# First unit of a fused attention, MLP and gated-convolution kernel in one written order, with whole float32 weights in its second layer

## The chip, the cores and the metric

The kernel runs on one core of a Trainium2 chip. The metric is the device time of one launch in microseconds: a median of 1182.4 us over three runs, from 1181.29 to 1183.06. The engines are named TensorE (PE in the rows; PEld are its weight loads), VectorE (DVE), ScalarE (ACT), GpSimd (POOL) and SyncE (SP, which issues the transfers).

## The reference

```python
# x (8, 8, 512, 64): batch, head, token, d; state (8, 8, 32, 64)
scores = x @ state.T / 8;  xread = softmax(scores) @ state          # tokens read the state
scores2 = state @ x.T / 8; sread = softmax(scores2) @ x             # the state reads the tokens
x = concat([xread, sread], axis=2)    # 544 rows per head, then the heads side by side: (8, 544, 512)
xn = (x - mean) / sqrt(var + 1e-6) * g_ln
x = x + relu(xn @ w_ch1) @ w_ch2      # w_ch1 (512, 2048), w_ch2 (2048, 512), read as below
h = relu(x @ w_in)                    # w_in (512, 1024)
out = h * sigmoid(conv3(h, conv_w)) @ w_out
```

`x`, `state` and the result are float32. The three weight matrices and `conv_w` arrive as float64 and are rounded to float32 on the chip before use.

## The kernel before

The work on the batch is cut into units. Units 0 to 7 are the 512 tokens of one batch element each; a unit numbered 8 holds the 256 state rows of all of them and runs before the last. A unit's layers are tiled into 16 slices `m` of 128 hidden columns. `L1(u, m)` is the first layer of a slice: since the tokens are weighted sums of 32 state rows per head, it multiplies the token weights (`AH`, `AL`) with the state already multiplied into the weights (`Z`), not the 512-column rows. `z_tiles` makes that `Z` from the state and a folded quarter `j` of w_ch1. `relu_parts` takes the ReLU out of the PSUM bank `ph` on ScalarE (`hH`, line 633) and its remainder on VectorE (`hL`, line 634). `L2(u, m, n)` adds the slice into the four PSUM banks `acc`; `residual` scales them by the norm's `rstd` and adds the tokens. For a product close to float32, `three` (lines 619 to 621) multiplies a high and a low part held as fp32r: high by high, high by low, low by high.

The weights arrive as raw 64-bit words. `round_1` (two ScalarE passes) and `round_2` (two VectorE passes, lines 205 and 206, here called a rounding pair, and a GpSimd addition, line 207) make float32 of them; `Converter.third` splits a rounded w_ch2 slice into its two parts, on ScalarE (line 239) and GpSimd (line 240). All 32 pieces (16 of w_ch1, 16 of w_ch2) are converted in the first unit, through three temporaries: `ctmp0`, `ctmp1` and a part of `XTt`. In that unit `z_first(j)` also folds the norm into a quarter of w_ch1: four float32 products with `gmean` on TensorE (line 609), four VectorE corrections (line 612), then the z products (line 585), and a store of the folded quarter to `w1d` in DRAM. Later units load it back through a ring of seven buffers (`pass_pairs`).

Beside a unit's products run the tasks of the next: `token_norm` of this unit, then `attend` of the next (scores, two softmaxes, state reads, token reads), one step in each gap between slices.

The order is set in two ways. The first steps (`START`) and everything from the second unit to the first steps of the last part are issued as written. The first unit's body is arranged by a scheduler, which moves instructions of different slices past each other on each engine's queue. A piece is converted when a product needs it, four places ahead (`need`, `AHEAD`).

## Time and profile before

| | us |
|---|---|
| median of three runs | 1182.4 |
| profiled execution | 1177.81 |
| its span, first to last instruction | 1176.0 |
| TensorE busy | 1125.9 (96%) |
| VectorE busy | 726.6 (62%) |
| ScalarE busy | 444.2 (38%) |
| GpSimd busy | 207.8 (18%) |

The profiled execution is 4.6 us shorter than the median of the timed runs; a difference between the kernels is worked out on the profiled one and then taken off the median. In the page's view of 40 slices of 29.4 us each, TensorE is busy for five to eight tenths of the first four slices and nine or more of nearly all others; GpSimd works in the first five slices and again in the last part alone. Shares of busy time over the whole span say little here, since the first 173 us and the rest have different limits.

### The profile page before, as it was taken

Reading aid. Unit: us, or ns where it says so; the run is one execution under the profiler, and the core shown is the slowest. Engines: PE = TensorE matmul, PEld = TensorE weight load, DVE = VectorE, ACT = ScalarE, POOL = GpSimd, SP = SyncE. Lnnn points to the kernel's source line nnn. Section 1 sums busy time; section 2 is a strip of 40 time slices with the busy share of each in tenths; the row PEclk is TensorE's granted clock in tenths of the full one; section 3 lists DMA queues with packets and bytes.
Section 4 is the critical chain, followed back from the end, with each engine's and each line's share of the span. In section 5 each row is a group of like instructions: output and inputs, shape, how many; then the busy total and the mean of one; then the engine's idle time right before and its main releaser. Section 6 shows DMA issues by size and latency. Waiting matters only on the chain.

```text
span 1176.0 us, 14628 instructions
## 1 busy us (share of the span) xinstructions
PE 1125.9 (96%) x5459; PEld 863.8 (73%) x5459; DVE 726.6 (62%) x1134; ACT 444.2 (38%) x788; POOL 207.8 (18%) x314
## 2 busy tenths in 40 slices
PE   5698899999999999999989999999999999999997
PEld 4365567777777777777767888788788888888885
DVE  4899666566566475565665622577677666666553
ACT  5665333323233233233233222565344434334332
POOL 2565400000000000000000000265433312213110
PEclk8699999999999999999999999999999999999999
DMA  9643533432243333334314124322112102100001
GB/s 298 206 171 108 158 96 105 108 95 90 72 109 85 81 111 76 78 120 108 95 56 107 38 101 155 119 72 90 37 54 72 37 37 80 37 36 36 1 37 45
DMA packets 129283, 106.31 MB, mean 90 GB/s; under 512 B 103332, under 2 KB 107452, under 8 KB 128188
## 3 DMA queue, kind: packets, MB, share of 16 engines
q1 hardware_dynamic: 129212, 105.37, 29.6%
q8 instruction: 43, 0.70, 0.2%
q14 instruction: 28, 0.23, 0.1%
HBM read 83.85 MB, written 21.50 MB: 90 GB/s over the span
## 4 chain that ended last, share of the span: by engine, by line
PE 80%; DVE 12%; ACT 3%; issue 2%; POOL 2%; SPq 0%; DMA 0%; ACTq 0%; DVEq 0%; POOLq 0%
PE acc L619 14%; PE acc L620 14%; PE acc L621 14%; PE ph L619 7%; PE ph L620 7%; PE ph L621 7%; PE pat L585 2%; PE pat L621 2%; PE pat L619 2%; PE pat L620 2%; PE pat L361 2%; PE ph L647 2%; DVE tn L500 1%; ACT bQ L488 1%; DVE ctmp L206 1%
## 5 line engine op out<-in xcount | busy, mean ns | idle before, releaser
L619 PE MATMUL acc<-hH,w 128*128 128x512 f32 (+1 forms) x576 | 221.6, 395 | 2.2 <-ACT hH L633 2.2
L620 PE MATMUL acc<-hL,w 128*128 128x512 f32 (+1 forms) x576 | 220.4, 383 | 1.8 <-DVE hL L634 1.7
L621 PE MATMUL acc<-hH,w 128*128 128x512 f32 (+1 forms) x576 | 220.1, 382 | 0.0
L634 DVE SCALAR_TENSOR_TENSOR hL<-ph,hH 128x512 fp32r<-128x512 f32 (+1 forms) x144 | 94.2, 657 | 183.4 <-ACT hH L633 183.2
L633 ACT ACTIVATE hH<-ph 128x512 fp32r<-128x512 f32 (+1 forms) x144 | 81.6, 569 | 208.9 <-PE ph L621 171.3
L619 PEld LDWEIGHTS acc<-hH,w 128*128 128x128 f32 x576 | 108.1, 188 | 54.5 <-issue 15.9
L1008 DVE SCALAR_TENSOR_TENSOR w<-w,cw,w 128x544 f32<-128x544 f32 x128 | 109.9, 860 | 38.0 <-POOL w L1006 36.2
L620 PEld LDWEIGHTS acc<-hL,w 128*128 128x128 f32 x576 | 109.2, 190 | 24.3 <-DVE hL L634 4.2
L621 PEld LDWEIGHTS acc<-hH,w 128*128 128x128 f32 x576 | 109.0, 189 | 21.7
L207 POOL TENSOR_TENSOR ctmp<-ctmp,AH 128x512 int32<-128x512 int32 x1 | 1.3, 1304 | 610.7 <-DVE ctmp L206 610.7
L619 PE MATMUL ph<-AH,ZH 128*128 128x512 f32 x256 | 104.3, 408 | 0.7 <-ACT ZH L594 0.7
L620 PE MATMUL ph<-AL,ZH 128*128 128x512 f32 x256 | 100.9, 394 | 0.0
L621 PE MATMUL ph<-AH,ZL 128*128 128x512 f32 x256 | 100.1, 395 | 0.0
L989 ACT ACTIVATE w<-w 128x544 f32<-128x544 f32 x64 | 42.1, 657 | 129.4 <-DVE w L1008 129.4
L996 DVE TENSOR_TENSOR w<-w,w 128x512 fp32r<-128x512 f32 x64 | 49.5, 774 | 42.9 <-ACT w L995 42.1
L990 DVE TENSOR_TENSOR w<-w,w 128x544 f32<-128x544 f32 x64 | 48.8, 762 | 39.5 <-ACT w L989 39.5
L619 PEld LDWEIGHTS ph<-AH,ZH 128*128 128x128 f32 x256 | 48.5, 190 | 19.5 <-issue 6.6
L995 ACT ACTIVATE w<-w 128x512 fp32r<-128x512 f32 x64 | 40.4, 631 | 52.4 <-DVE w L990 47.4
L1006 POOL TENSOR_SCALAR w<-w,cw 128x544 f32<-128x544 f32 x64 | 47.7, 746 | 61.8 <-ACT w L1002 58.4
L621 PEld LDWEIGHTS ph<-AH,ZL 128*128 128x128 f32 x256 | 48.2, 189 | 11.8 <-issue 0.8
L620 PEld LDWEIGHTS ph<-AL,ZH 128*128 128x128 f32 x256 | 48.6, 190 | 9.7
L997 POOL COPY w<-w 128x32 f32<-128x32 f32 x64 | 17.5, 273 | 177.5 <-DVE w L990 177.5
(439 smaller groups left out, 2182.0 us busy)
## 6 DMA issues: line engine op xcount, KB each, us to landing
r<-w1d SPq DMA_DIRECT2D x64, 512.0 KB, 4.5
out_dram<-w SPq DMA_DIRECT2D x34, 256.0 KB, 2.2
w<-in_moe_w_ch_dram SPq DMA_DIRECT2D x16, 512.0 KB, 8.0
r<-in_moe_w_ch_dram SPq DMA_DIRECT2D x16, 512.0 KB, 4.9
x2d<-XT SPq DMA_DIRECT2D x8, 1024.0 KB, 4.9
bP<-in_x_dram SPq DMA_DIRECT2D x112, 64.0 KB, 2.5
bP<-in_x_dram SPq DMA_DIRECT2D x28, 256.0 KB, 3.8
w1d<-r SPq DMA_DIRECT2D x8, 512.0 KB, 2.6
```

The costliest lines, as they stand in the source:

```text
L361: T.matmul(xr[ql], s[:, 2 * g + ql], a, start=i == 0, stop=i == 2)
L619: T.matmul(o, lh, rh, start=first, stop=False)
L620: T.matmul(o, lh, rl, start=False, stop=False)
L621: T.matmul(o, ll, rh, start=False, stop=last)
L633: A.activation(h, p, AF.Relu)
L634: V.scalar_tensor_tensor(l, p, 0.0, f32(h), op0=ALU.max, op1=ALU.subtract)
L989: A.activation(c, c, AF.Sigmoid)
L990: V.tensor_tensor(c, c, h[:, 1 : SEQ + 1], op=ALU.mult)
L995: A.activation(g[:, 0], c[:, :S], AF.Copy)
L996: V.tensor_tensor(g[:, 1], c[:, :S], f32(g[:, 0]), op=ALU.subtract)
L1006: G.tensor_scalar(c, h[:, 0:SEQ], cw[:, f : f + 1], 0.0, op0=ALU.mult, op1=ALU.add)
L1008: V.scalar_tensor_tensor(c, h[:, k : k + SEQ], cw[:, k * FF + f : k * FF + f + 1], c, op0=ALU.mult, op1=ALU.add,)
```

## The change

The first unit no longer runs under the scheduler. Its work is cut into streams of pieces, and one string `START` names the stream that gives the next piece: `a` and `b` are the two halves of the rounding, `z` the folding of a quarter, `P` the products, `S` the state softmaxes and reads, `L` the token reads, `T` the attention of the second unit, `N` the norm of the first, `d` loads. Each stream draws its PSUM banks from a list of its own. The string ends with the z step of the second unit.

The second layer of the first unit takes a rounded w_ch2 slice whole: one float32 product per block with a float32 `hH`, without `hL` and without the split. Two rounded slices share one tile (`pair2`), so that all 16 are kept. The second unit splits them, slices 0 and 1 ahead of its first product and slice `m + 2` behind the second layer of slice `m`, ScalarE for the high part and VectorE for the low one; a split slice goes to a slot whose content is used up (`slot2`).

```diff
-    hH = new("hH", [2, S], F32R)
-    hL = new("hL", [2, S], F32R)
+
+    hid = {c: new(f"h{c}", [2, S], F32 if c == "H" else F32R) for c in "HL"}
...
-    START = "s0w1ws0a1bab01ca01cabcabc"
+    START = "0ss1aba0b101a0ab1aSbaSbazbLLzPSNbPaSaSPbbSaPabSSPSadNbddddNaPabaNbzPbzPaNbaPNbNPPbTPPTTTaaabadbTbPTaabdzPbzPTTPabbTaaPTbbPaaTPbTTdabTTzPPbabzPTTPadTPbaPTPbPPPPPPTdPNTT"
...
     def z_first(j):
 
 
-        for q in range(KC):
-            need(1, KC * j + q)
         w = rounded[2 * j : 2 * j + 2]
         vp = bank()
...
+        yield
         z_tiles(0, j, w)
         for g in range(2):
             nc.sync.dma_start(w1d[j, g], flat(w[g]))
+        yield
...
     def hidden(m):
-        return hH[:, m % 2], hL[:, m % 2]
-
-    def relu_parts(m, p):
+        return hid["H"][:, m % 2], hid["L"][:, m % 2]
+
+    def relu_parts(u, m, p):
+        if u == 0:
+            A.activation(hid["H"][:, m % 2], p, AF.Relu)
+            return
+        if (u, m) == (1, 0):
+            hid["H"] = new("hH", [2, S], F32R)
         h, l = (t[:, : p.shape[1]] for t in hidden(m))
         A.activation(h, p, AF.Relu)
         V.scalar_tensor_tensor(l, p, 0.0, f32(h), op0=ALU.max, op1=ALU.subtract)
...
     def L2(u, m, n):
         h, l = (t[:, :n] for t in hidden(m))
         for d in range(KC):
             c = slice(P * d, P * d + P)
-            three(acc[d][:, :n], w2[m][:, 0, c], w2[m][:, 1, c], h, l, m == 0, m == M1 - 1)
+            if u == 0:
+                T.matmul(acc[d], whole2[m][:, c], h, start=m == 0, stop=m == M1 - 1)
+            else:
+                three(acc[d][:, :n], w2[m][:, 0, c], w2[m][:, 1, c], h, l, m == 0, m == M1 - 1)
+
+    def split_w2(m):
+
+        w = w2[m] = new(slot2(m), [2, DM], F32R)
+        A.activation(w[:, 0], whole2[m], AF.Copy)
+        V.tensor_tensor(w[:, 1], whole2[m], f32(w[:, 0]), op=ALU.subtract)
...
+    w2, whole2, pair2 = {}, {}, {}
+
+    def slot2(m):
+        return f"w2_{(m + 7) % M1}" if m < M1 - 1 else "w2_e"
...
-    AHEAD = 4
-
-    def need(a, m):
-        i = place_of[a, m]
-        conv_a.ensure(min(i + AHEAD, conv_a.total - 1))
-        return conv_a.done[i]
...
         if a == 2:
-            return None
+            if m % 2 == 0:
+                pair2[m // 2] = new(f"w2_{m // 2 - 1}" if m else "w2_e", [2, DM])
+            whole2[m] = pair2[m // 2][:, m % 2]
+            return whole2[m].rearrange("p (k c) -> p k c", c=P)
         if m % 2 == 0:
             rounded.append(new(f"r{RAWS + m // 2 % 2}", [2, S]))
-        if m + RAWS < M1:
-            load_weight(place_of[1, m + RAWS])
         return rounded[m // 2][:, m % 2].rearrange("p (k c) -> p k c", c=P)
...
+    def firsts():
+        for _ in range(conv_a.total):
+            conv_a.first()
+            yield
+
+    def seconds():
+        for i, (a, m) in enumerate(order):
+            conv_a.second()
+            if a == 1 and m + RAWS < M1:
+                load_weight(place_of[1, m + RAWS])
+            yield
+
+    def firsts_made():
+        for j in range(KC):
+            yield from z_first(j)
+
+    def products_start():
+        L1(0, 0)
+        yield
+        for m in range(M1):
+            if m < M1 - 1:
+                L1(0, m + 1)
+                yield
+            L2(0, m, S)
+            yield
+        yield from residual(0, S)
+        z_step(1, 0)
+
+    def loads_start():
+        load_state(1)
+        yield
+        for m in range(LATE, M1):
+            load_weight(place_of[2, m])
+            yield
+        pass_pairs(RING)
...
+    streams = {
+        "s": (state_start(), acc),
+        "0": (tokens_start(0, x0T[0], sets[0]), acc),
+        "1": (tokens_start(1, x0T[1], sets[1]), acc),
+        "a": (firsts(), acc),
+        "b": (seconds(), acc),
+        "L": (reads_start(), acc),
+        "S": (states_start(), pat),
+        "z": (firsts_made(), pat),
+        "P": (products_start(), pat),
+        "T": (attend(1), pat),
+        "N": (token_norm(0), pat),
+        "d": (loads_start(), acc),
+        "w": (warm_steps(), acc),
+    }
+    turn = {}
+    steps = {c: s[0] for c, s in streams.items()}
+    for c in START:
+        banks["held"], banks["free"], banks["next"] = None, streams[c][1], turn.get(c, 0)
+        next(steps[c], None)
+        turn[c] = banks["next"]
+    banks["free"], banks["held"] = pat, None
...
+    splits = {(1, m): [m + 2] for m in range(M1 - 2)}
+    for m in range(2):
+        split_w2(m)
+
+
+    L1(1, 0)
+    units = [*range(1, NB - 1), NB, NB - 1]
...
-            if u == 0:
-                w2[m] = need(2, m)
             L2(u, m, n)
-            while u == 0 and made and made[0][0] < 12 and made[0][0] == m:
-                gap(m)
+            for k in splits.get((u, m), ()):
+                split_w2(k)
```

VectorE up to the first `ZL`, the last thing that the first layer of the first unit waits for. Before:

```order
L315 TENSOR_TENSOR bV_388<-pat_83,rm_57_384 128x128
L315 TENSOR_TENSOR w_13_60_394<-pat_84,rm_59_390 128x128
L326 TENSOR_REDUCE XTt_65<-pat_83 128x2x32
L326 TENSOR_REDUCE XTt_65<-pat_84 128x2x32
L205 TENSOR_SCALAR ctmp_78_500<-ctmp_78_500 128x512
L206 SCALAR_TENSOR_TENSOR ctmp_78_500<-r_43_254,ctmp_78_500 128x512
L612 SCALAR_TENSOR_TENSOR r_40_245<-r_40_245,gcol_72,pat_84 128x512 x2
L612 SCALAR_TENSOR_TENSOR r_45_284<-r_45_284,gcol_72,pat_84 128x512 x2
L595 TENSOR_TENSOR ZL_71_462<-pat_83,ZH_70_461 128x512
L595 TENSOR_TENSOR ZL_71_462<-pat_84,ZH_70_461 128x512
```

And now:

```order
L285 TENSOR_REDUCE m_53_313<-pat_84 128x1
L286 TENSOR_SCALAR m_53_313<-m_53_313 128x1
L208 TENSOR_SCALAR ctmp_47_288<-ctmp_47_288 128x512
L209 SCALAR_TENSOR_TENSOR ctmp_47_288<-w_0_20_119,ctmp_47_288 128x512
L613 SCALAR_TENSOR_TENSOR r_38_217<-r_38_217,gcol_72,pat_83 128x512 x2
L613 SCALAR_TENSOR_TENSOR r_45_276<-r_45_276,gcol_72,pat_83 128x512 x2
L208 TENSOR_SCALAR XTt_65<-XTt_65 128x4x128
L209 SCALAR_TENSOR_TENSOR XTt_65<-w_1_21_121,XTt_65 128x4x128
L598 TENSOR_TENSOR ZL_58_361<-pat_84,ZH_57_360 128x512
L598 TENSOR_TENSOR ZL_58_361<-pat_83,ZH_57_360 128x512
```

Before, the state reads' scaling (L313 to L326) and the pieces of later quarters stand ahead of L612; now state softmaxes and the first w_ch2 pieces stand around it, and what belongs to the state reads comes behind the first `ZL`.

TensorE, the second layer's second slice of the first unit. Before, the 12 instructions of `three`:

```order
L619 MATMUL acc_77<-hH_63,w_1_63_416 128x512
L619 MATMUL acc_78<-hH_63,w_1_63_416 128x512
L619 MATMUL acc_79<-hH_63,w_1_63_416 128x512
L619 MATMUL acc_80<-hH_63,w_1_63_416 128x512
L620 MATMUL acc_77<-hL_64,w_1_63_416 128x512
L621 MATMUL acc_77<-hH_63,w_1_63_416 128x512
L620 MATMUL acc_78<-hL_64,w_1_63_416 128x512
L621 MATMUL acc_78<-hH_63,w_1_63_416 128x512
L620 MATMUL acc_79<-hL_64,w_1_63_416 128x512
L621 MATMUL acc_79<-hH_63,w_1_63_416 128x512
L620 MATMUL acc_80<-hL_64,w_1_63_416 128x512
L621 MATMUL acc_80<-hH_63,w_1_63_416 128x512
```

And now, with the first layer of the slice after it:

```order
L328 MATMUL pat_84<-ident_70,w_13_73_452 128x128
L665 MATMUL acc_77<-hH_63,w_e_318 128x512
L665 MATMUL acc_78<-hH_63,w_e_318 128x512
L665 MATMUL acc_79<-hH_63,w_e_318 128x512
L665 MATMUL acc_80<-hH_63,w_e_318 128x512
L816 MATMUL pat_83<-ident_70,cbuf 128x24
L483 MATMUL pat_83<-bQ_389,ones_71 128x512 x2
L622 MATMUL ph_82<-AH_32_173,ZH_57_360 128x512
L623 MATMUL ph_82<-AL_33_174,ZH_57_360 128x512
L624 MATMUL ph_82<-AH_32_173,ZL_58_361 128x512
L622 MATMUL ph_82<-AH_32_173,ZH_57_360 128x512
L623 MATMUL ph_82<-AL_33_174,ZH_57_360 128x512
```

A float32 product is one row here and a pair of instructions on the machine, as in line 609.

SyncE where the first unit ends. Before:

```order
L574 DMA r_169_1183<-w1d 128x1024
L574 DMA r_170_1185<-w1d 128x1024
L158 DMA bP_1207<-in_x_dram 32x16x32 x8
L574 DMA r_177_1324<-w1d 128x1024
L673 DMA x2d<-XT_31_172 128x2048
L574 DMA r_178_1326<-w1d 128x1024
L574 DMA r_191_1429<-w1d 128x1024
L574 DMA r_192_1431<-w1d 128x1024
```

And now:

```order
L617 DMA w1d<-r_135_863 128x1024
L191 DMA w_15_149_959<-in_moe_w_ch_dram 128x1024
L161 DMA bP_969<-in_x_dram 32x16x32 x8
L129 DMA s_in_66<-in_state_dram 32x2x32 x8
L144 DMA s_raw_67<-in_state_dram 32x64 x8
L577 DMA r_156_1068<-w1d 128x1024
L577 DMA r_157_1070<-w1d 128x1024
L577 DMA r_158_1072<-w1d 128x1024
L577 DMA r_159_1074<-w1d 128x1024
```

The loads of the second unit's first four folded halves stood early and spread out; now the eight token, eight state-column and eight state-row transfers for later units (`bP`, `s_in`, `s_raw`) stand just ahead of all seven.

## Rows read from the trace of the kernel before

**Rows 1.** Busy time by stretch: PE, PEld, DVE, ACT, POOL, granted clock, DMA share, GB/s.
```profile
24.00:61.40 37.40, 24.14 (x103) 13.53 (x103) 31.29 (x53) 25.43 (x48) 14.82 (x11) 0.67 0.74 230
61.40:172.90 111.50, 102.65 (x474) 69.39 (x470) 88.16 (x134) 50.27 (x86) 50.48 (x36) 0.97 0.43 127
172.90:254.40 81.50, 81.13 (x427) 60.07 (x419) 48.64 (x86) 25.79 (x45) 0.00 (x0) 1.00 0.34 92
```

**Rows 2.** Waits of PE up to 175 us: total us, times, longest.
```profile
PE pat L456 <- DVE bU L450: 7.5, 1, 7.5
PE pat L290 <- ACT w L284: 4.3, 1, 4.3
...
PE pat L273 <- DVE bQ L369: 3.9, 1, 3.9
```

**Rows 3.** Timeline of PE: start us, length us, instruction.
```profile
48.39 1.98 PE L300 MATMUL pat<-XT,bV 128*64 128x128 f32 x16
...
61.47 0.50 PE L619 MATMUL ph<-AH,ZH 128*128 128x512 f32 x1
...
172.91 0.50 PE L619 MATMUL acc<-hH,w 128*128 128x512 f32 x1
...
177.13 0.39 PE L619 MATMUL acc<-hH,w 128*128 128x512 f32 x1
...
179.88 0.69 PE L480 MATMUL pat<-bQ,ones 128*128 128x512 f32 x2
```

**Rows 4.** Timeline of DVE between 31 and 38 us.
```profile
31.73 0.68 DVE L206 SCALAR_TENSOR_TENSOR ctmp<-w,ctmp 128x512 int32<-128x512 int32 x1
...
35.47 0.41 DVE L205 TENSOR_SCALAR ctmp<-ctmp 128x512 int32<-128x512 int32 x1
35.92 1.66 DVE L206 SCALAR_TENSOR_TENSOR ctmp<-w,ctmp 128x512 int32<-128x512 int32 x1
37.50 0.68 DVE L282 TENSOR_REDUCE m<-pat 128x1 f32<-128x512 f32 x1
```

**Rows 5.** Timeline of POOL in the same stretch.
```profile
35.63 1.40 POOL L207 TENSOR_TENSOR XTt<-XTt,w 128x512 int32<-128x512 int32 x1 [0.63 <-DVE XTt L206]
37.71 1.27 POOL L207 TENSOR_TENSOR ctmp<-ctmp,w 128x512 int32<-128x512 int32 x1 [0.69 <-POOL XTt L207]
```

**Rows 6.** Groups of DVE up to 172.9 us: count, busy us, mean ns, idle before.
```profile
L205 DVE TENSOR_SCALAR ctmp<-ctmp 128x512 int32<-128x512 int32 x22 | 14.8, 675 | 1.5 <-ACT ctmp L199 1.5
L206 DVE SCALAR_TENSOR_TENSOR ctmp<-r,ctmp 128x512 int32<-128x512 int32 x11 | 12.2, 1107 | 0.2
...
L634 DVE SCALAR_TENSOR_TENSOR hL<-ph,hH 128x512 fp32r<-128x512 f32 x17 | 11.5, 682 | 8.5 <-ACT hH L633 8.5
...
L206 DVE SCALAR_TENSOR_TENSOR XTt<-r,XTt 128x512 int32<-128x512 int32 x5 | 4.4, 885 | 0.1
```

**Rows 7.** Groups of POOL up to 172.9 us.
```profile
L207 POOL TENSOR_TENSOR ctmp<-ctmp,w 128x512 int32<-128x512 int32 x11 | 16.6, 1512 | 11.4 <-issue 6.0 <-DVE ctmp L206 4.1 <-POOL XTt L207 0.7
L240 POOL TENSOR_TENSOR w<-ctmp,w 128x512 fp32r<-128x512 f32 x11 | 15.2, 1392 | 1.5 <-ACT w L239 1.5
```

**Rows 8.** Timeline of ACT at the first piece.
```profile
16.30 0.63 ACT L445 ACTIVATE bU<-bU 128x512 f32<-128x512 f32 x1 [3.22 <-DVE bU L444]
16.83 0.64 ACT L199 ACTIVATE ctmp<-r 128x512 f32<-128x512 f32 x1
```

**Rows 9.** Timeline of PE at a folding step's products and what follows.
```profile
103.21 3.59 PE L609 MATMUL pat<-r,gmean 128*128 128x512 f32 x8
106.24 1.48 PE L619 MATMUL acc<-hH,w 128*128 128x512 f32 x4
107.56 0.39 PE L620 MATMUL acc<-hL,w 128*128 128x512 f32 x1
```

**Rows 10.** Timeline of SP: transfers issued.
```profile
45.48 5.13 SPq L126 DMA_DIRECT2D s_in<-in_state_dram  x7
...
120.09 6.53 SPq L158 DMA_DIRECT2D bP<-in_x_dram  x8
```

**Rows 11.** DMA issues of the page: count, KB each, median us from issue to landing.
```profile
r<-w1d SPq DMA_DIRECT2D x64, 512.0 KB, 4.5
```

More of the change, by code (lines that the diff above doesn't have):

```diff
@@ L767, in warm @@
         for _ in range(n):
-            T.matmul(acc[3], hL[:, 1, :P], hL[:, 0], start=True, stop=True)
+            T.matmul(acc[3], hid["L"][:, 1, :P], hid["L"][:, 0], start=True, stop=True)
     warm(WARM)
-    steps = {
-        "s": state_start(),
-        "0": tokens_start(0, x0T[0], sets[0]),
-        "1": tokens_start(1, x0T[1], sets[1]),
-    }
-    conv_steps = {"a": conv_a.first, "b": conv_a.second, "c": conv_a.third}
-    for c in START:
-        if c == "w":
-            warm(1)
-        elif c in steps:
-            next(steps[c], None)
-        else:
-            conv_steps[c]()
-    tc_start.close()
-    load_state(1)
-    banks["free"] = pat
-    round_1(craw, c0)
-    round_2(craw, c0)
     def states_start():
         starts = [work, {"V": spare[5], "R": spare[6], "s": "1"}]
-        E2Ts, z2s = [], []
+        E2s, z2s, srzs = [], [], []
         for g in range(2):
@@ L884 @@
         made = []
[L885 to L888 removed]
+        if u < NB:
+            made += [(0, u, 1), (3, u, 2), (7, u, 3)]
             if u != LAST:
[L890 removed]
+                made.append((10, LAST if follow == NB else follow, 0))
         def gap(m):
             if made and m >= made[0][0] and banks["held"] is None:
[L894 to L898 removed]
+                z_step(*made.pop(0)[1:])
             else:
                 next(tasks, None)
[L902 to L910 removed]
         for m in range(M1):
@@ L913 @@
                 L1(u, m + 1)
-            if u == 0 and m == 3:
-                for k in range(LATE, M1):
-                    load_weight(place_of[2, k])
-            if u == 0 and m == M1 - 4:
-                pass_pairs(RING)
             if u == LAST:
@@ L946 @@
                 gap(m)
-        residual(u, n)
+        for _ in residual(u, n):
+            pass
         if u != LAST:
@@ L952, in place @@
     def place(m, shape, dt=F32):
-        return new(f"w2_{m}", shape, dt)
+        return new(slot2(m), shape, dt)
     hb = [place(m, [HB]) for m in range(3)]
```

56 lines of the change are left out of this document (24 added, 32 removed).

## The prediction

> **What bounds the kernel now.** I read the stretches first. From the start of the second unit on, TensorE is busy for 81.13 of 81.50 us with its clock fully granted, while VectorE, ScalarE and GpSimd have room: there only TensorE's own work counts. Before that it is different: between 24 and 61.4 us TensorE is busy for 24.14 of 37.40 us, VectorE for 31.29, and between 61.4 and 172.9 us TensorE sits idle for 111.50 - 102.65 = 8.85 us beside a VectorE at 88.16 [rows 1]. The waits of TensorE say for whom: in the opening for VectorE's and ScalarE's softmax (7.5 and 4.3 us), later for the transpose of the next unit's tokens (3.9 us) [rows 2]. So the opening is bound by VectorE in a round trip with the others, and everything after it by TensorE. Two marks on TensorE's line measure the change: its first product of the first layer, at 61.47 us, and its first product of the second layer in the second unit, at 172.91 us [rows 3]. From the second mark on both kernels do the same work, but for the splits that now lie in the second unit. The saving is what the second mark moves.
>
> **First mark: the shortened way to the first product.** Before, the conversions, token reads, state softmaxes, state reads and transposes stand ahead of the first folding step (L609). In the new order VectorE needs less before the first ZL: six rounding pairs (L208, L209), 17 operations on 512 columns and half a dozen small ones. The state reads and their transposes come after.
>
> The 512-column operations take 0.68 us [rows 4]: 17 x 0.68 = 11.6 us; the small ones I put at 1.2. A rounding pair alone takes 0.41 + 0.68 = 1.09 us, but beside a GpSimd addition its second half took 1.66 us [rows 4, 5]; over all 32 pairs the means are 0.675 and, weighted over temporaries, about (22 x 1.107 + 10 x 0.885)/32 = 1.04, together 1.71 us [rows 6]. The excess of 0.62 us a pair came beside 48 GpSimd operations, 32 additions and 16 subtractions (L240) of 1.4 us [rows 7]. The change takes the 16 subtractions off GpSimd; with 32 left I keep two thirds, 0.42, and put a pair at 1.5 us: 6 x 1.5 = 9.0.
>
> The first piece is read by ScalarE at 16.83 us, at once, after a wait for something else [rows 8]; in the new order it is read sooner, and I let VectorE begin at 14. Sum: 14 + 9.0 + 11.6 + 1.2 = 36 us, and 3 us for the three places where it waits for an answer (transposes and copy of the token weights; the last addition and the tail of L610; L588 and the copy ZH). First product at 39 instead of 61.5 us: **-22.5 us**. Bounds: 14 + 6.5 + 12.9 + 1 = 34.5 with free pairs, and 16.8 + 6 x (1.09 + 0.98) + 12.9 + 5 = 47 with every pair held as in [rows 4]; -27 to -14.5.
>
> **Second mark: what TensorE has to do between.** It was 172.91 - 61.47 = 111.4 us [rows 3].
>
> The second layer of the first unit turns from three fp32r products per block into one float32 product, which the machine issues as two instructions. Twelve fp32r instructions of a slice run from 177.13 to 179.88 us, 2.75 us [rows 3]. The float32 products of the same shape are those of L609: eight instructions from 103.21 us; the four after them are spaced 0.23 us and the next begins at 107.56, so the eight hold the engine until about 106.64, 3.43 us, or 0.43 each [rows 9]. Eight such instructions make a new slice: 3.43 - 2.75 = 0.68, times 16: **+10.8 us**. The change thus adds work to the engine that bounds everything else; what it removes there is nothing. It could be as low as 0, if TensorE waits for VectorE anyway.
>
> The state reads, moved behind the first mark, are TensorE's too: 16 instructions of L300 took 1.98 us [rows 3] at the granted clock of 0.67 in that stretch [rows 1], so some 1.0 us at full clock; with the transposes some 1.9 us for each half: **+3.8 us**.
>
> VectorE loses 16 corrections of the hidden rows (L634, 0.68 us, 11 us in all [rows 6]), ScalarE and GpSimd the 16 splits (GpSimd 16 x 1.4 us [rows 7]). None of this ends on the path by itself. It gives the air that lets VectorE keep up with an earlier TensorE, and the wait L620 had for hL is gone.
>
> The waits: TensorE's own work in this stretch is about 94 us by start-to-start distances: 18 slices of the first layer with 6 fp32r instructions, 16 of the second with 12, and 16 more, 316 x 0.23 = 73, three L609 groups 10, and some 11 for z products, scores, transposes and reads. So some 17 of the 111.4 us are lost: 8.9 idle, about 3.3 at a clock of 0.97 [rows 1], the rest small handovers. For the new order I walked TensorE's and VectorE's queues side by side. Lost there: at each of the three later folding steps (L610), which wait for the last of four additions, about 2 us, 6 in all; 2 at the scores of the second half (L276), because bP can be loaded only after the state read of the first half, and its eight transfers take 6.5 us to issue [rows 10], with the transpose (L372) holding every later VectorE instruction behind it; and 3.2 at the end of the unit. There the token read, the copy XT and the z step follow the last L665 in one chain, and VectorE has four products and four additions of the residual ahead of ZL. With a slow clock of 2 us at the start and the small handovers of 3 to 4 that is again 17. I take **no difference**, from -9 (half of these waits hidden) to +10 (each folding step exposed in full).
>
> SP is passed too: 24 small transfers stand before the seven ring loads that the second unit's z step reads. Eight of the first kind took 6.53 us, seven of the second 5.13; with the third alike that is some 18 us in all, and a ring load lands 4.5 us after its issue [rows 10, 11]. They are released by the state read of the second half, which I put 23 us before the z step: just hidden.
>
> **The second unit.** It gains 14 copies on ScalarE and 14 subtractions on VectorE, 0.68 us each like L634 [rows 6]: 9.5 us beside 48.64 of 81.50 us busy [rows 1]. Behind each stands the correction hL of the next slice, due only 4 us later. I take +0.4 us, from 0 to +3.
>
> **The sum.** -22.5 + 10.8 + 3.8 + 0 + 0.4 = -7.5 us. The profiled execution lasted 1177.8 us (span 1176.0), 4.6 less than the median of 1182.4; taken off the median: **1174.9 us**.
>
> **A rule against it.** The second half of a pair waited 0.98 us beside an addition, while an operation that reads a PSUM bank did not (L282, 0.68, with the addition of 37.71 us under it) [rows 4, 5]. The Trainium skill (GPSIMD Engine Reference, Specifications) says that GpSimd's SBUF interfaces are shared with VectorE, with contention for instructions in a two-port mode or with two SBUF inputs. The rows agree; by the rule alone any pair that follows a pair would be held, in whatever order it is issued. The result of that is the second rival below.
>
> **The rivals.**
> *The air is worth more.* VectorE keeps ahead of TensorE, since GpSimd has a third fewer operations and the new order often puts a PSUM operation behind a pair. Then the folding steps hardly wait, and the loss falls from 17 to 9: 1174.9 - 8 = 1167 us. For it: VectorE drops from 88 busy us by 11 in the long stretch. Against it: 26 pairs still lie there.
>
> *VectorE's lane sets the end; slower.* In a fixed queue, a folding step is a round trip: handover and addition 2.0, the tail of L610 0.9, four L613 2.7, L588 1.0, ZH and ZL 1.3, about 8 us; the new order puts a single slice of 3.4 us into it. Exposed in full three times that is 13.8 instead of 6, and with each of the 26 pairs held for 0.98 instead of 0.42 us VectorE's queue grows by 14.6, of which perhaps 9 shows at L276 and at the residual: 17 us above the forecast, 1192 us. It decides against the change from about 10 us of extra loss on. For it: the opening before behaved just so. Against it: 8 us of folding lie beside first-layer products too.
>
> *The order does not do what it says.* If the early start is only turned into waiting later (VectorE's work as a whole shrinks by 11 us, TensorE's grows by 10.8), the second mark stays where it was: 1182 us.
>
> **Numbers.** The forecast (a saving of 3 to 12 us) 0.53, the first rival 0.23, no gain 0.11, slower 0.13. The forecast's own range is 1170 to 1179. A range that holds 8 in 10 goes from 1164 to 1183. A difference of 0.2%, 2.4 us, is about what a measurement can tell from none: faster 0.76, within 0.11, slower 0.13.
>
> **What would show it.** The first L622 near 39 us, and the first L622 on acc near 165; slices of L665 spaced 3.4 us; a pair near 1.5 us; waits of L610 and L588 of about 2 us each time and of 3 us before the first ZH of the second unit; the rest of the trace the same length, within 1 us. A first product later than 47 us, or more than 27 us lost between the marks, would prove the forecast wrong.

## The result, and the profile after

The changed kernel takes **1165.2 us** (median of 4 runs, 1163.5 to 1166.6) against 1181.9 us of the kernel before beside it; the ratio is 0.9864, 95% interval 0.9837 to 0.9892. Timed again with more runs of the kernel before, it is 1165.2 against 1181.3 us, 0.9871 (0.9851 to 0.9891). It is faster, as forecast, but by some 16 us where 7.5 were forecast.

Its profiled execution lasted 1166.6 us with a span of 1164.8, so the two profiled spans differ by 11.2 us. I first account for these 11.2 us. The rest of the 16.7 lies between each profile and the median of its kernel: the profiled execution before was 4.0 us shorter than the 1181.9, the one after 1.4 us longer than the 1165.2. The end of the experiments looks for where that comes from.

Each line number after the change is a few higher (L619 is now L622, L609 now L610, L585 now L588). TensorE's timeline after the change, with the first mark, the second mark and the last slice of the first unit between them (start, length, instruction):

```profile
37.73 0.50 PE L622 MATMUL ph<-AH,ZH 128*128 128x512 f32 x1 [0.63 <-ACT ZH L597]
...
141.89 7.03 PE L665 MATMUL acc<-hH,w 128*128 128x512 f32 x16
148.35 1.02 PE L364 MATMUL pat<-AH,s_H 128*128 128x512 f32 x2
149.22 0.63 PE L364 MATMUL pat<-AH,s_L 128*128 128x512 f32 x2
...
156.80 0.50 PE L622 MATMUL acc<-hH,w 128*128 128x512 f32 x1
```

The first mark came from 61.47 to 37.73, the second from 172.91 to 156.80 [rows 3]: -23.7 and -16.1 us. Between them lie 119.1 us in place of 111.4. The last two slices, 16 instructions, begin at 141.89. The next two records follow at 148.35 and the two after them at 149.22; instructions of this kind are spaced 0.23 us, so the 16 hold the engine until about 148.75, 6.9 us. That is 3.4 us a slice, as forecast. VectorE's timeline has the third mark, the first residual operation of the second unit, before and after; one row of each:

```profile
248.60 2.74 DVE L670 TENSOR_TENSOR tn<-acc,rs 128x512 f32<-128x512 f32 x4 [3.40 <-PE acc L621]
```

```profile
237.13 2.76 DVE L687 TENSOR_TENSOR tn<-acc,rs 128x512 f32<-128x512 f32 x4 [3.78 <-PE acc L624]
```

So the second unit went from 75.7 us to 80.3 (+4.6), and what is left from 927.4 to 927.7 (+0.3). -23.7 + 7.6 + 4.6 + 0.3 = -11.2 us. The stretches that answer to [rows 1], in the same columns:

```profile
24.00:37.70 13.70, 11.96 (x56) 6.54 (x56) 10.92 (x19) 9.92 (x20) 4.42 (x4) 0.84 0.93 238
37.70:156.80 119.10, 113.13 (x449) 57.37 (x449) 89.52 (x150) 58.59 (x105) 36.27 (x28) 1.00 0.53 169
156.80:238.30 81.50, 79.24 (x395) 58.15 (x388) 51.57 (x91) 31.77 (x57) 0.00 (x0) 0.98 0.31 89
238.30:319.80 81.50, 81.16 (x419) 60.05 (x418) 48.07 (x85) 25.83 (x45) 0.00 (x0) 1.00 0.33 92
```

Between the marks TensorE is idle for 6.0 us in place of 8.9, its clock is granted in full (0.97 before), and GpSimd is busy for 36 us in place of 50. The second unit has 2.3 us idle and a clock of 0.98, the third is as the second was before. The first three of TensorE's waits between the marks, all short (total us, times, longest), answer to [rows 2]:

```profile
PE ph L622 <- ACT ZH L597: 2.1, 4, 0.7
PE pat L328 <- DVE w L318: 1.8, 1, 1.8
PE pat L610 <- DVE bU L384: 1.1, 1, 1.1
```

### The profile page after: what moved, and what is told of

Its sections match the earlier page's. It is cut to its first block, busy times and chain, and to the rows that moved or that the text cites. A ratio compares the mean times of both kernels' runs of the same rounds, so it can differ in the third digit from the quotient of the medians.

```text
span 1164.8 us, 14520 instructions
## 1 busy us (share of the span) xinstructions
PE 1129.4 (97%) x5393; PEld 848.4 (73%) x5393; DVE 716.3 (61%) x1134; ACT 441.4 (38%) x788; POOL 182.3 (16%) x298
## 5 line engine op out<-in xcount | busy, mean ns | idle before, releaser
L642 DVE SCALAR_TENSOR_TENSOR hL<-ph,hH 128x512 fp32r<-128x512 f32 (+1 forms) x128 | 83.4, 654 | 173.7 <-ACT hH L641 173.4
L622 PE MATMUL acc<-hH,w 128*128 128x512 f32 (+1 forms) x480 | 189.5, 395 | 0.0
L624 PE MATMUL acc<-hH,w 128*128 128x512 f32 (+1 forms) x480 | 182.4, 380 | 0.0
L623 PE MATMUL acc<-hL,w 128*128 128x512 f32 (+1 forms) x480 | 182.2, 380 | 0.0
L641 ACT ACTIVATE hH<-ph 128x512 fp32r<-128x512 f32 (+1 forms) x128 | 72.7, 568 | 197.2 <-PE ph L624 159.8
L1064 DVE SCALAR_TENSOR_TENSOR w<-w,cw,w 128x544 f32<-128x544 f32 x128 | 109.7, 858 | 35.1 <-POOL w L1062 33.3
L622 PEld LDWEIGHTS acc<-hH,w 128*128 128x128 f32 x480 | 90.7, 189 | 44.4 <-issue 15.2
L622 PE MATMUL ph<-AH,ZH 128*128 128x512 f32 x256 | 106.8, 417 | 2.1 <-ACT ZH L597 2.1
L624 PEld LDWEIGHTS acc<-hH,w 128*128 128x128 f32 x480 | 90.4, 188 | 18.1
L623 PEld LDWEIGHTS acc<-hL,w 128*128 128x128 f32 x480 | 90.7, 189 | 16.7 <-DVE hL L642 0.3
L210 POOL TENSOR_TENSOR ctmp<-ctmp,AH 128x512 int32<-128x512 int32 x1 | 1.3, 1312 | 600.0 <-DVE ctmp L209 600.0
L622 PEld LDWEIGHTS ph<-AH,ZH 128*128 128x128 f32 x256 | 48.3, 189 | 23.5 <-issue 8.9
L665 PE MATMUL acc<-hH,w 128*128 128x512 f32 x112 | 50.4, 594 | 0.0
```

Source lines behind the costliest of these rows:

```text
L622: T.matmul(o, lh, rh, start=first, stop=False)
L623: T.matmul(o, lh, rl, start=False, stop=False)
L624: T.matmul(o, ll, rh, start=False, stop=last)
L641: A.activation(h, p, AF.Relu)
L642: V.scalar_tensor_tensor(l, p, 0.0, f32(h), op0=ALU.max, op1=ALU.subtract)
L665: T.matmul(acc[d], whole2[m][:, c], h, start=m == 0, stop=m == M1 - 1)
```

## The experiments

All numbers of this table are from the profiled execution of each kernel, in us: the first mark, the way to the second, the second unit (second mark to its first residual operation), the span; and the median of its runs. What is left after the second unit is 927.0 to 928.9 everywhere. The medians were taken at different times, each beside the kernel before, whose own median went from 1179.0 to 1181.9.

| kernel | first mark | between | second unit | span | median |
|---|---|---|---|---|---|
| before (first profile) | 61.5 | 111.4 | 75.7 | 1176.0 | 1179.0 to 1181.9 |
| after | 37.7 | 119.1 | 80.3 | 1164.8 | 1165.2 |
| order_three | 37.1 | 141.7 | 75.7 | 1181.8 | 1184.7 |
| float32_alone | 62.8 | 116.9 | 80.2 | 1187.8 | 1189.6 |
| gsplit | 36.0 | 118.9 | 80.5 | 1163.8 | 1165.4 |
| three_no_hl | 36.3 | 127.6 | 75.8 | 1166.8 | 1168.8 |
| after_hl | 37.0 | 134.2 | 78.8 | 1178.3 | 1180.0 |
| hl_late | 35.4 | 124.4 | 78.7 | 1166.6 | 1170.7 |
| three_late | 34.9 | 157.3 | 75.7 | 1195.2 | 1198.6 |
| three_free | 36.2 | 116.3 | 80.3 | 1160.6 | 1161.9 |
| tail_splits | 36.6 | 119.1 | 75.7 | 1160.3 | 1162.2 |
| tail_early | 37.0 | 117.4 | 75.9 | 1159.1 | 1160.6 |
| tail_warm3 | 35.1 | 117.4 | 75.9 | 1156.6 | 1159.0 |

**The change again, and each half of it alone.** The repeat (after2) has no edit.

> The changed kernel again, unaltered, timed beside the kernel before in more rounds, since the two profiled executions differ by 11.2 us of span and the medians by 16.7. If the medians are the truer measure, the saving is again 15 to 18 us; if the two first runs of the kernel before were untypical, it is 11 to 13.

Measured: 16.1 us below the kernel before by the medians; its span is 1165.1 us, its marks lie within 0.3 us of the first profile's. The medians' 16 us are confirmed.

The order alone undoes the other half (and has the splits made at conversion again, by ScalarE and GpSimd):

```diff
...
-            if u == 0:
-                T.matmul(acc[d], whole2[m][:, c], h, start=m == 0, stop=m == M1 - 1)
-            else:
-                three(acc[d][:, :n], w2[m][:, 0, c], w2[m][:, 1, c], h, l, m == 0, m == M1 - 1)
+            w = conv_a.done[place_of[2, m]]
+            three(acc[d][:, :n], w[:, 0, c], w[:, 1, c], h, l, m == 0, m == M1 - 1)
...
```

> The new written order alone: the first unit's second layer keeps its three rounded products and its split weights, made at conversion by ScalarE and GpSimd as before. Theory (the order gives the start, and the spared rounding work of the lanes gives the shorter stretch between the marks): the first mark stays near 37.7 us, but the 16 splits and the 16 lower parts of the hidden rows come back on lanes that the stretch waits for, so that although TensorE has 10.8 us less to do, the stretch stays at 115 to 121 us and the whole at 1160 to 1168 us. Rival (the order alone takes out the waits, the lanes have room): the stretch is 108 to 110 us, the second unit loses its 4.6 us of splits too, and the whole is 1150 to 1156 us.

Measured: 1184.7 us, ratio 1.0036 (1.0024 to 1.0048), slower than before. Neither theory held. The first mark is as early as in the changed kernel, but 22.6 us more than there lie between the marks, though TensorE has 10.8 us less to do. VectorE's longest wait in that stretch (total us, times, longest), and the row of its part up to the first unit's residual, in the columns of [rows 1]:

```profile
DVE hL L637 <- ACT hH L636: 27.7, 15, 3.8
```

```profile
37.10:169.00 131.90, 107.39 (x456) 70.55 (x457) 93.52 (x153) 62.58 (x112) 58.47 (x44) 0.90 0.41 125
```

TensorE is idle for 24.5 us there, and its clock is 0.90.

In the kernel before, VectorE's wait at hL was 8.5 us in 4 places.

The whole weights alone put the float32 product into the old order, with the splits in the second unit and no hL in the first:

```diff
...
-            three(acc[d][:, :n], w2[m][:, 0, c], w2[m][:, 1, c], h, l, m == 0, m == M1 - 1)
+            if u == 0:
+                T.matmul(acc[d], whole2[m][:, c], h, start=m == 0, stop=m == M1 - 1)
+            else:
...
```

> The whole float32 weights alone, under the order and scheduler of the kernel before, with the splits in the second unit. Theory that the order gives the gain: first mark near 61 us as before, the stretch between the marks 111 to 122 us, the second unit 4 to 5 us dearer, the whole 1184 to 1196 us, slower than before. Rival that the lane work taken out of the first unit is what gave the gain: the first mark a few us earlier, the stretch 104 to 110 us although TensorE has 10.8 us more to do, and the whole 1172 to 1181 us.

Measured: 1189.6 us, ratio 1.0070 (1.0051 to 1.0088): the first theory, slower. Between the marks it took 5.5 us more than before, not 10.8; the second unit cost 4.5. So each half alone loses, 3 and 8 us, and both together gain 16. The string `START` was written for the changed kernel; an order written for rounded products was not tried, so "the order alone" means this string alone. The next runs look for what the order needs of the other half.

**The lower parts hL.** Taken out of order_three, with TensorE's products kept (the one with hL reads zeros):

```diff
-        V.scalar_tensor_tensor(l, p, 0.0, f32(h), op0=ALU.max, op1=ALU.subtract)
+        if u:
+            V.scalar_tensor_tensor(l, p, 0.0, f32(h), op0=ALU.max, op1=ALU.subtract)
```

> The new order with three rounded products (as in order_three), without the 16 lower parts hL of the hidden rows in the first unit: the correction is left out there, the product with it reads zeros that were written at the start, so TensorE and the other lanes do the same work as in order_three. Theory (hL stands in VectorE's queue waiting for a product of TensorE, 25.7 us of waiting in order_three, and the attention's and the rounding's own work stands behind it): most of the lost time goes, first mark to first residual 95 to 108 us in place of 131.9, the whole 1148 to 1160 us. Rival (only VectorE's 11 us of busy time count): at most 11 us less than order_three, 1173 to 1185 us. Second rival (the 16 subtractions on GpSimd that slow VectorE): no change beyond 3 us, 1181 to 1185.

Measured: 1168.8 us, 15.9 less than order_three; between the marks it is 14.1 less. That is more than the 11 us of busy time that went, so the rival of busy time fell; but from the first mark to the first unit's residual it is 117.6 us, not the 95 to 108 of the theory, so something else holds it too (below). The same step the other way, hL put into the changed kernel:

```diff
-            A.activation(hid["H"][:, m % 2], p, AF.Relu)
+            h, l = hidden(m)
+            A.activation(h, p, AF.Relu)
+            V.scalar_tensor_tensor(l, p, 0.0, h, op0=ALU.max, op1=ALU.subtract)
             return
```

> The changed kernel with the 16 lower parts hL put back on VectorE in the first unit; the correction is made from the unrounded rows and read by nobody, so TensorE, ScalarE and GpSimd do the same work as in the changed kernel. Theory (their place in VectorE's queue is what costs): first mark to first residual grows from 108.7 us by 10 to 20, the whole 1175 to 1187 us. Rival (VectorE has the room: it was busy for 80.9 of 108.7 us and would be for 92): at most 3 us more, 1165 to 1168.

Measured: 1180.0 us, 14.9 more than the changed kernel, 15.1 more between the marks: the theory. One place shows how. VectorE, GpSimd and TensorE of after_hl near 60 us (a row's bracket has the idle time before it and what ended it):

```profile
56.76 1.22 DVE L503 TENSOR_TENSOR tn<-XT,pat 128x1024 f32<-128x1024 f32 x1 [0.86 <-PE pat L483]
60.70 0.69 DVE L638 SCALAR_TENSOR_TENSOR hL<-ph,hH 128x512 fp32r<-128x512 f32 x1 [2.72 <-ACT hH L637]
61.31 0.42 DVE L208 TENSOR_SCALAR XTt<-XTt 128x512 int32<-128x512 int32 x1
61.76 0.69 DVE L209 SCALAR_TENSOR_TENSOR XTt<-r,XTt 128x512 int32<-128x512 int32 x1
...
62.59 1.28 POOL L210 TENSOR_TENSOR r<-XTt,r 128x512 int32<-128x512 int32 x1 [5.23 <-ACT w L203]
...
63.92 1.20 PE L610 MATMUL pat<-r,gmean 128*128 128x512 f32 x2 [3.33 <-POOL r L210]
```

and the same place in the changed kernel:

```profile
56.50 1.22 DVE L503 TENSOR_TENSOR tn<-XT,pat 128x1024 f32<-128x1024 f32 x1 [0.86 <-PE pat L483]
57.63 0.42 DVE L208 TENSOR_SCALAR XTt<-XTt 128x512 int32<-128x512 int32 x1
58.09 0.69 DVE L209 SCALAR_TENSOR_TENSOR XTt<-r,XTt 128x512 int32<-128x512 int32 x1
...
57.60 3.79 PE L610 MATMUL pat<-r,gmean 128*128 128x512 f32 x8
```

VectorE stands at hL for 2.72 us, until ScalarE has written hH. The rounding pair behind it needs nothing of that; it starts 3.7 us later than in the changed kernel. The addition on GpSimd reads what the pair writes and starts as the pair ends (the view names a ScalarE pass as its releaser, but that ended at 61.8), and the folding product that reads the sum stops TensorE for 3.33 us. In the changed kernel the eight L610 run through. Over the stretch to the first unit's residual TensorE has this wait in three places, where the changed kernel has none:

```profile
PE pat L610 <- POOL r L210: 5.4, 3, 3.3
```

Is it the place in the queue, or just 11 us more work? The same 16 operations were put one step later:

```diff
     def L2(u, m, n):
         h, l = (t[:, :n] for t in hidden(m))
+        if u == 0:
+            V.scalar_tensor_tensor(l, ph[m % 2], 0.0, h, op0=ALU.max, op1=ALU.subtract)
```

> As after_hl, with the same 16 lower parts on VectorE, but each put into its queue one step later, ahead of the second-layer slice that would read it and not behind the first-layer product that makes it. Theory (the loss of 14.9 us is that of a queue in order: VectorE arrives early and waits for TensorE with other work behind): most of it is gone, 1165 to 1171 us, and VectorE's wait for hH falls from 21.6 us to under 8. Rival (what costs is the 11 us of busy time on VectorE): 1175 to 1181 us as in after_hl.

Measured: 1170.7 us: the theory. Of 14.9 us 9.4 came back, with the same work on VectorE (90.67 us from the first mark to the first unit's residual in after_hl, 89.97 here) and its wait at hL down from 21.6 us to

```profile
DVE hL L663 <- ACT hH L636: 7.1, 2, 4.1
```

Between the marks 9.8 of 15.1 us came back. So some two thirds of the price of hL here is its place in VectorE's queue; what the remaining 5 us are was not taken apart.

In three_late, which is order_three with that shift, hL really is read:

```diff
...
+        if u == 0:
+            V.scalar_tensor_tensor(l, ph[m % 2], 0.0, f32(h), op0=ALU.max, op1=ALU.subtract)
         for d in range(KC):
...
+            w = conv_a.done[place_of[2, m]]
+            three(acc[d][:, :n], w[:, 0, c], w[:, 1, c], h, l, m == 0, m == M1 - 1)
...
```

> As order_three (new order, three rounded products, splits at conversion), with each hL of the first unit put into VectorE's queue one step later, ahead of the slice that reads it. Theory of the queue: the 15.9 us that hL costs there come back in good part, 1169 to 1177 us, but for slices that now wait for hL. Rival (busy time): 1181 to 1186 us.

Measured: 1198.6 us, outside both expectations. TensorE now waits for it (first mark to the first unit's residual):

```profile
PE acc L623 <- DVE hL L659: 33.8, 13, 3.9
```

Early it blocks VectorE's queue, late it blocks TensorE's. Neither of the two places tried in this order is cheap; the float32 product does without it.

**What the longer slices cost.** The float32 product replaced by three rounded ones without any lane's work for them. The real weights are left out; a constant tile `ones` stands in their place:

```diff
-                T.matmul(acc[d], whole2[m][:, c], h, start=m == 0, stop=m == M1 - 1)
+                three(acc[d], ones, ones, h, l, m == 0, m == M1 - 1)
```

> The changed kernel with the first unit's second layer as three rounded products in place of one float32 product, but with none of the lower parts: the weights are left out (a constant tile stands in their place) and hL reads zeros, so no lane does more than in the changed kernel and TensorE does 10.8 us less. Theory (TensorE's longer slices cost in full, since it waits for 6.8 us only between the marks): first mark to first residual 97 to 101 us in place of 108.7, the whole 1153 to 1157 us. Rival (the written order ties so much lane work to each slice that shorter slices only wait): 105 to 109 us, the whole 1161 to 1166 us.

Measured: 1161.9 us; between the marks 116.3 in place of 119.1 us, from the first mark to the first residual 106.4 in place of 108.7. The rival held: 10.8 us of TensorE's work are worth 2.8 us of time between the marks. That TensorE need not wait for the weights here is no part of it, since in the changed kernel no wait at L665 appears. Shorter slices let it wait longer and more often; its waits of three_free up to the residual begin with

```profile
PE pat L610 <- DVE bU L384: 2.4, 1, 2.4
PE pat L328 <- DVE w L318: 2.0, 1, 2.0
```

where the changed kernel has 1.1 and 1.8, and the clock is 0.97 in place of 1.00. The difference to three_no_hl, 127.6 - 116.3 = 11.3 us, is the price of the 16 splits at conversion on ScalarE and GpSimd. Whether that is ScalarE's queue, GpSimd's, or the operations that slow each other was not taken apart. The trace of three_no_hl has one lead, a wait of ScalarE's first rounding pass for GpSimd's split (L243), which holds one of the three temporaries until it has read it:

```profile
ACT ctmp L202 <- POOL w L243: 11.0, 6, 3.8
```

In three_free the like wait (for GpSimd's addition, L210) is 2.7 us. A kernel with more temporaries would tell; none was run.

**The second unit.** The subtraction of the splits was moved from VectorE to GpSimd:

```diff
-        V.tensor_tensor(w[:, 1], whole2[m], f32(w[:, 0]), op=ALU.subtract)
+        G.tensor_tensor(w[:, 1], whole2[m], f32(w[:, 0]), op=ALU.subtract)
```

> The changed kernel with the subtraction of each split in the second unit on GpSimd in place of VectorE. Theory (the second unit's 4.6 us come from the splits standing in VectorE's queue ahead of the attention's own steps): 2 to 4.6 us come back, 1160.5 to 1163.5 us. Rival (the splits cost by their mere number, or GpSimd is late with them or slows VectorE beside it): 1165 to 1168 us, with waits for the split weight at the products that read it.

Measured: 1165.4 us, the second unit still 80.5: the rival, though without the waits for the split weight that it named. In the changed kernel a split stands in VectorE's queue just ahead of an operation of the norm (bQ, L478), for which TensorE waits; then its clock falls:

```profile
176.56 0.68 DVE L673 TENSOR_TENSOR w<-w,w 128x512 fp32r<-128x512 f32 x1
177.16 0.68 DVE L478 TENSOR_TENSOR bQ<-rs,bQ 128x512 fp32r<-128x512 f32 x1
...
177.90 0.50 PE L483 MATMUL pat<-bQ,ones 128*128 128x512 f32 x1 [1.29 <-DVE bQ L478]
...
179.13 0.63 PE L622 MATMUL acc<-hH,w 128*128 128x512 f32 x1
179.56 0.63 PE L623 MATMUL acc<-hL,w 128*128 128x512 f32 x1
```

At full clock the same instructions take 0.39 us and follow each other by 0.23, here 0.63 and 0.43. By the row of the second unit above, the idle 2.3 us and the clock of 0.98 (some 1.6 us, an estimate from that share) make up most of the 4.6. With GpSimd doing the subtraction, VectorE's own operation beside it grows, and TensorE waits for that:

```profile
174.88 1.27 POOL L673 TENSOR_TENSOR w<-w,w 128x512 fp32r<-128x512 f32 x1 [3.12 <-ACT w L672]
175.08 1.61 DVE L478 TENSOR_TENSOR bQ<-rs,bQ 128x512 fp32r<-128x512 f32 x1
...
176.75 0.50 PE L483 MATMUL pat<-bQ,ones 128*128 128x512 f32 x1 [1.63 <-DVE bQ L478]
```

0.68 became 1.61 us, and TensorE's wait of 1.29 became 1.63. This is the contention that the prediction weighed. The Trainium skill (GPSIMD Engine Reference, Specifications) says that GpSimd shares its SBUF interfaces with VectorE, whose instructions with two SBUF inputs contend for them. L478 has two, and its 1.61 us agree.

The splits were then moved to where VectorE had waited for the last products of the first unit:

```profile
DVE tn L687 <- PE acc L665: 12.6, 1, 12.6
```

```diff
+        early = {14: range(6), 15: range(6, 11), 16: range(11, M1)}
         for m in range(M1):
+            for k in early.get(m + 1, ()):
+                split_w2(k)
...
-            for k in splits.get((u, m), ()):
-                split_w2(k)
```

> The changed kernel with all 16 splits ahead of the last three slices of the first unit, where VectorE waited 12.6 us for the last product and ScalarE had four operations left, and none in the second unit. Theory (the second unit's 4.6 us come from the splits there): the second mark stays at 156 to 158 us, the second unit takes 75.7 us again, the whole 1160 to 1162 us. Rival (the splits delay the hidden rows and the residual by as much at the end of the first unit): 1164 to 1168 us.

Measured: 1162.2 us. The second unit is 75.7 us again, and the way between the marks is unchanged, 119.1: the theory. The spans differ by 4.5 us (what is left after the second unit was 1.2 us longer, which I can't explain, and the first mark came 1.1 earlier), the medians by only 2.9, as the changed kernel's profiled execution is 1.4 us longer than its median. Next, the last token read, the ring loads and the folding step of the second unit before the last slices:

```diff
-    START = "...TPbaPTPbPPPPPPTdPNTT"
+    START = "...TPbaPTPbdPPPTPPPPNTT"
...
+            if m == M1 - 1:
+                z_step(1, 0)
             L2(0, m, S)
             yield
         yield from residual(0, S)
-        z_step(1, 0)
```

> As tail_splits, and the last token read, the ring loads and the folding step of the second unit are put ahead of the last slices of the first unit, so that TensorE need not wait for the copies XT and ZH between the units. Theory: first residual to second mark 7 to 8.5 us in place of 9.6 with the first residual later by the moved work, the whole 1159.5 to 1161.5 us. Rival (the folding step's transfers or its lane work arrive late there): 1162 to 1165 us.

Measured: 1160.6 us, between the marks 117.4: the theory, within its range for the whole. Taking away most of what TensorE lost between the units was worth 1.7 us.

**The rest of the 16 us.** Three further profiles of the kernel before, unaltered, were taken.

> The kernel before, unaltered, for a second profiled execution: the first one (1177.8 us) was the fastest of all that were timed, while the changed kernel's two were above its median. Theory: this one is longer by 2 to 5 us, and the difference lies in one stretch at a lower granted clock in the first two units. Rival: the difference is spread evenly over the span, and then it says nothing of the change.

> The kernel before, one more profiled execution: the two so far lasted 1177.8 and 1176.8 us, the timed ones 1179 to 1182 in the median. If a longer one comes (1180 us or more), its stretches show where the difference lies: theory, a stretch of the first unit at a lower granted clock; rival, spread over the span.

> As before_c, a further profiled execution of the same kernel, for the same question: a time of 1180 us or more with the excess between the first mark and the first residual, or spread over the span.

Measured: 1176.8, 1179.7 and 1183.0 us (spans 1175.0, 1177.9, 1181.2). The expectation of a longer one failed at before_again and held at before_d; there the excess lies at a lower clock, as the theory had it, but ahead of the first mark. Between the marks all four have 109.7 to 111.5 us, the second unit is 75.7 in each. The first mark is at 61.5, 62.6, 62.5 and 65.9 us: most of the difference to before_d lies in the opening. TensorE's first scores in the first profile, and the stretch from 14 to 16 us in the columns of [rows 1]:

```profile
12.81 2.00 PE L436 MATMUL pat<-sbd,w 128*128 128x64 f32 x16 [0.65 <-DVE sbd L414]
14.65 1.95 PE L436 MATMUL ph<-sbd,w 128*128 128x64 f32 x16
```

```profile
14.00:16.00 2.00, 2.00 (x21) 2.00 (x20) 1.12 (x2) 0.00 (x0) 0.48 (x1) 1.00 1.03 416
```

and in before_d, with its first mark:

```profile
12.37 3.67 PE L436 MATMUL pat<-sbd,w 128*128 128x64 f32 x16 [0.52 <-DVE sbd L414]
15.83 3.62 PE L436 MATMUL ph<-sbd,w 128*128 128x64 f32 x16
...
65.89 0.50 PE L619 MATMUL ph<-AH,ZH 128*128 128x512 f32 x1
```

```profile
14.00:16.00 2.00, 2.00 (x11) 2.00 (x11) 0.00 (x0) 0.00 (x0) 0.23 (x1) 0.50 1.01 385
```

In one execution the granted clock is 1.00 there (2.4 GHz), in the other 0.50 (1.2 GHz), and VectorE's second softmax, with the rounding behind it, starts 2.9 us later. The Trainium skill (TensorE: Matmul & The Clock Gate, Part 1: The HAM clock gate) says that how much of a kernel's beginning runs at the lower clock varies from run to run. The four profiles agree: the two scores took 2.0 and 2.0 us in two of them, 2.0 and 2.9 in before_c, 3.7 and 3.6 in before_d. The clock of the scores doesn't explain everything: before_again has the full clock and still a first mark 1.1 us behind that of the first profile. That first profile, on which the prediction rests, has the earliest first mark of the four, though before_again has the shorter span; with before_d as the kernel before, the spans differ by 16.4 us. before_c, at 1179.7 us, lies within the range of the medians (1179.0 to 1181.9); it is 1.9 us longer than the first profile, 1.0 of them before the first mark and 1.0 after the second unit. The timed executions point the same way without showing the place: of those of the kernel before whose mean clock is on record, all of 1182 us or more have 0.972 to 0.978, all below 1179 us 0.979 or more.

The changed kernel varies in its opening too. Its first scores took 3.67 and 3.62 us, half clock, in both of its profiles, and so they did in after_hl and tail_early, which share its opening: first marks at 37.0 to 37.7 us. In gsplit, three_free and tail_splits, with the same opening, a part of them ran at full clock, first marks at 36.0 to 36.6; in hl_late both did, first mark at 35.4. So some 2 us of a difference between two of these medians can be the opening. The changed order has none of the idle products that the order before puts between the transposes. They were put back into tail_early:

```diff
-    START = "0ss1aba0b101a...
+    START = "0ssww1wwwaba0b101a...
```

> As tail_early, with five idle products of TensorE put back into the opening (two ahead of the second half's transposes, three behind them), as the kernel before has there; the changed order has none. Four profiled executions of the kernel before differ in the first scores (2.0 us each at full clock, 3.67 us at half) and in the first mark (61.5 to 65.9 us), the changed kernel's ran at half clock in both. Theory: the scores run at full clock, up to 3.3 us come off the first mark and 1.5 to 3.3 off the whole, 1157 to 1159 us. Rival: VectorE has other pieces to do there and is not waiting for the scores, or the idle products delay the transposes: 1160 to 1162 us.

> As tail_warm3 with six idle products behind the transposes in place of three, which cover the whole gap up to the first scores. Theory: as there, and the clock is full in every execution, 1156.5 to 1158.5 us. Rival: the scores stand behind the idle products and start later, 1160 to 1163 us.

Measured: 1159.0 us for both (tail_warm6 1158.96), ratio to the kernel before 0.9813 (0.9797 to 0.9829) and 0.9810 (0.9793 to 0.9827): the theory for tail_warm3, at its upper end, and 0.5 us above it for tail_warm6. The first scores of tail_warm3 and its first mark:

```profile
12.29 2.00 PE L439 MATMUL pat<-sbd,w 128*128 128x64 f32 x16 [0.68 <-DVE sbd L417]
14.12 1.95 PE L439 MATMUL ph<-sbd,w 128*128 128x64 f32 x16
...
35.09 0.50 PE L622 MATMUL ph<-AH,ZH 128*128 128x512 f32 x1 [0.64 <-ACT ZH L597]
```

The first mark is 1.9 us earlier than in tail_early, the median 1.6 us lower. That the idle products gave the full clock is likely and not shown: one profile of each kernel had it, but so had hl_late without them, and before_d had two of them and half clock. These two are the fastest versions found, some 6 us below the changed kernel (1159.0 and 1165.2).

## Why the prediction was right in sign and wrong in size

Term by term, the saving was forecast at 7.5 us and measured at 16.7: 1.2 more at the first mark, 7.0 more between the marks, 4.2 less in the second unit, 0.3 less in what is left, and 5.5 more from the reference.

**First mark: right, in part by luck.** -22.5 us were forecast, -23.7 measured against the first profile. VectorE's first pair began at 13.3 us where I put 14, and the six pairs took 7.3 us where I put 9.0; its waits on the way were 5.0 us where I put 3. These errors cancel. A rounding pair took 1.30 us over all 32 (41.5 us of L208 and L209 on 512 columns), where I put 1.5 and the kernel before had 1.73 (55.2 us; the 1.71 of the prediction left out the mean of L205 on `XTt`).

**Second mark: the step that failed is "The waits ... I take no difference".** The prediction put +10.8 (float32) and +3.8 (state reads) between the marks and left 17 us of lost time as it was, +14.6 in all; +7.6 was measured. By its own 94 us of work and these two terms, 10.5 us are lost after the change and not 17. Of the losses that it listed for the new order, the 6 us at the folding steps (L610) turned out as 1.1, the 2 at L276 as none, and the 2 of a slow clock as none, the clock being 1.00. The first rival, that the air is worth more, had named the direction, at a chance of 0.23. That its 1167 us lies so near the measured 1165.2 is luck, since the misses in the second unit and in the reference, which it shared, nearly cancel.

The runs show what stands in the place of that step. From the kernel before to the changed one, the stretch between the marks went from 111.4 to 141.7 us by the order alone, by 14.1 down to 127.6 without hL, by 11.3 down to 116.3 without the splits at conversion, and up to 119.1 with the float32 product. So the terms aren't a sum of engine times. The state reads were work as forecast (16 instructions of L303 took 1.09 us), but were not tried by themselves. The 10.8 us of float32 were work, as the slices of 3.4 us show, but only 2.8 us of time (three_free); the prediction had that as its lower bound, 0 "if TensorE waits for VectorE anyway", and did not use it. And the operations taken off the lanes, of which it said "None of this ends on the path by itself", were worth 25.4 us in the new order. I had treated hL as busy time; some two thirds of its price is that it stops VectorE's queue. With hL back, the waits at the folding steps that I had forecast are there (after_hl, 5.4 us in three places).

**The second unit: mis-sized.** +0.4, from 0 to +3, was forecast; +4.6 measured and found to be the splits (tail_splits). I had looked at how late a split could be and at VectorE's share of busy time, not at what stands behind the split: an operation of the norm, for which TensorE stops and loses its clock.

**The end of the first unit: not contradicted.** 3.2 us lost there were forecast; 1.7 came back when most of that was moved (tail_early). What is left there was not sized.

**The no-gain rival** was real for the order alone: it moves the first mark by 24.3 us and still ends 3.5 us later than before.

**The reference: a second step that failed.** "Taken off the median" assumed that both kernels' medians lie as far above their profiled executions. They did not: the kernel before was profiled 4.0 us below the median beside which the result was taken, the changed kernel 1.4 above its own, 5.5 us of the 16.7 together. The opening of the kernel before varied by 4.4 us in four profiles, and the one that the changed kernel shares with six others by some 2 in eight, which is enough for such distances. But before_c, the one profile near a median of the kernel before, owes to its opening only 1.0 of the 1.9 us by which it exceeds the first, and none was caught at 1181 to 1182 us or at the changed kernel's median. How much of the 5.5 us is the opening stays open.

## What to carry to other kernels

An operation on a queue that runs in order can cost more by what stands behind it than by what it takes: before adding or removing one, read which lane it waits for and who waits for the next item. When the order is written by hand, don't add up engine times per stage; build the one kernel in which the term is left out. And before a profiled execution is taken as the reference, compare its opening with a second one.

## What the runs showed of the hardware

The granted clock in the opening was 1.00 in some executions of a kernel and 0.50 in others for the same instructions (2.00 and 3.67 us); hl_late and three_late had 2.00 and 1.95 without idle products, the changed kernel and tail_early half clock. With five idle products the clock was full in the one profile taken, and that kernel's five runs lay within 1.2 us; before_d had two idle products and half clock. A VectorE subtraction of 128 x 512 with both inputs in SBUF took 0.68 us alone and 1.61 beside one of GpSimd.
